# TensorE operands on 64-byte starts, and one step per hand-over between engines, in a two-stage GLU plus FFT kernel

## The chip, the core and the metric

One core of a Trainium2 chip runs one program. Its engines work in parallel and each takes its own instructions in order: TensorE (PE: matmuls, and PEld, the load of the stationary operand before each), VectorE (DVE), ScalarE (ACT), GpSimd (POOL) and SyncE (SP, which here issues nearly all DMAs; SPq is its queue). They wait for each other through semaphores. The metric is the device time of one execution in microseconds (us).

## The reference

```python
x = A_x                                     # 1 x 2048 x 576, float32
xn = layernorm(x)
# A: 2-D FFT over (2048, 576), times w_r + i w_i, and back
y = irfft2(rfft2(xn, axes=(-2, -1)) * (w_r + 1j * w_i), s=(2048, 576))
# B: gated linear unit, F = 4608
g = xn @ w_gate                             # 2048 x 4608
u = xn @ w_up
z = (sigmoid(g) * u) @ w_down               # 4608 -> 576
out = x + y + z
```

## The kernel before

**Splits.** Matmuls read float32r. A value is split in two: ACT copies it rounded (`hi`), DVE subtracts that from the value (`lo`), and a product is three matmuls, hi x hi, lo x hi, hi x lo. So nearly every operand passes from ACT to DVE to PE. The helper is `split` (L134: ACT in L135, DVE in L136).

**First stage: h = sigmoid(g) * u.** The tokens are in two halves p, the features in 36 blocks f of 128. After four blocks worked plainly, `unit(f, p)` forms g and u of one block and half by seven products of sums (a 2x2 scheme with seven multiplications), each of seven matmuls of 512 columns (L352). The moving operands lie in tiles `X0...` for p = 0 (pool x0, at the upper end of the on-chip memory, "right") and `X1...` for p = 1 (pool x1, from the lower end), the weights in `w`. In the built program every X0 tile starts 32 bytes behind a multiple of 64, every X1 tile on one. PSUM banks are A, B and E; B is copied out by ACT (L395, L401) between products, and the fourth product needs the copy of L401 to be done. Beside the matmuls, one piece at each of seven places of a unit, run: `make_w` (splits of the next weights, L205 on ACT, L207 on DVE, with differences of blocks in L227 to L231), `export` (sums of h on DVE, L429 to L438, stored to DRAM as `ss`), and `make_t` (the same for w_down: `wd` to `tP`, L455 ACT, L457 DVE, stored to DRAM as `ts`).

**Second stage: the down projection in 252 steps.** `seq` lists (j, p, k): seven products j, two halves p, 18 blocks k. Step n takes a 128x512 block `sf` from DRAM (`fetch`, ten steps ahead, in a ring of eight buffers), splits it to `sp` (`cut`, four steps ahead, six buffers) and does 12 matmuls of 288 columns (L955): for each of four token tiles m three, into PSUM tile `m`, with moving operand `tt` (24 buffers; in the built program all 32 bytes behind a multiple of 64). After the last k of a sum, `evac` adds tile m to the accumulators `acc` and `u` (L885).

**The FFT runs beside these steps** as chains, 16 in each of three phases; a chain begins every 4.4 steps (`RATE`) and goes on by one `yield` per step. Phase 1 (`phase1b`, from step 3): normalise, transposes `pf`, products `pd` (290 columns) and `pa`, out to DRAM `sc1`. Phase 2 (from step 82): load `x2`, split, products `pb` (L772), ACT copies `sw` (L774, L775), DVE multiplies with the weights (L779, L780) and adds (L781), split `zh`/`zl`, products `pc` (L790), ACT copy `u`, out to `sc2`. Phase 3 (from step 163): load, split, `py`, `pz`, `pe` (L844), added to `acc`. Two double PSUM tiles `pp` serve them all. The 290-column operands of the FFT have rows of 1160 bytes and so start at changing multiples of 8 bytes.

**Order.** The code above records instructions; the layer under it then orders them on each engine by its own plan, so what stands on an engine is not the code's order exactly.

Of the kernel before, what the change touches and what calls it, by code (L numbers as in the profile page):

```python
# [56 lines left out]
def _constants():  # L57
# [4 lines left out]
    t = np.zeros((P, 2, 5, NQ), np.float32)  # L62
    for e, v in ((0, np.cos(ang)), (1, -np.sin(ang))):
        m = np.zeros((HD + 1, NQ))
        m[:, :KD] = v
        if e == 0:
            m[HD] *= 0.5
        else:
            m[0] = m[HD] = 0.0
            m[:, 256] = m[:, 288] = 0.0  # L70
        hi, lo = _split(m)
        for part, w in ((0, hi), (1, lo)):
            t[:, e, 2 * part] = w[:P]
            t[:, e, 2 * part + 1] = w[P:2 * P]
        t[:3 * FR, e, 4] = np.concatenate([hi[2 * P:], hi[2 * P:], lo[2 * P:]])
    out["cf"] = t.reshape(P, 10 * NQ)

# [46 lines left out]
def spectral_glu_kernel(ctx: ExitStack, tc: tile.TileContext, x, w_r, w_i, w_gate, w_up, w_down, out):  # L124
# [47 lines left out]
    first = ExitStack()  # L172
    xps = [first.enter_context(tc.tile_pool(name="x0", bufs=1, side="right", reuse_waits="tile")), pool1("x1")]
# [46 lines left out]

    def make_w(f):
# [3 lines left out]
        yield from parts(new_w(f, 0, 3), raw[:, 1:])  # L225

        nc.vector.tensor_tensor(raw[:, 3::-3], raw[:, :2], raw[:, 3::-3], op=OP.subtract)  # L227
# [68 lines left out]
    def new_rem(p, c, what):  # L296
        XR[p, c] = run.tile([P, TPC, 2, 3, REM], F32R, tag="rab"[0] + "ab"[c], name=f"rm{what}{p}{c}")
# [117 lines left out]
    def export(k, p):  # L415
# [10 lines left out]
        s = run.tile([P, 3, CW], F32, tag="s", name=f"s{k}_{p}")  # L426
        S1, S2, S4 = (s[:, i] for i in range(3))
# [10 lines left out]
        nc.vector.tensor_tensor(S4, A12, S2, op=OP.subtract)  # L438
        put("P3", S4)
        yield  # L440

    def make_t(k):

        ws = []
        for i in range(2):
            w = run.tile([P, D], F32, tag="r" + "ab"[i], name=f"wd{2 * k + i}")
# [6 lines left out]
        def put(what, src):  # L453
            t = run.tile([P, 2, HD], F32R, tag="tt", name=f"t{what}{k}")
# [23 lines left out]
    nc.scalar.dma_start(f32(idr), con["id"])  # L478
# [101 lines left out]
    TS, FA, CA = NPR + 6, 10, 4  # L580
# [28 lines left out]
    for i, u in enumerate(UNITS):  # L609
# [35 lines left out]
        if p == 1:  # L645
            sides += [make_t(k) for k in range(NPR) if 4 + k * 5 // 3 == f]
# [16 lines left out]
    spp = pool2("sp")  # L663
# [26 lines left out]

    def phase1b(t):
# [10 lines left out]
        eo = pool.tile([P, 2, HD + 2], F32, tag="eo", name=f"eo{t}")  # L702
        for e, op in ((0, OP.add), (1, OP.subtract)):
            nc.vector.tensor_tensor(eo[:, e, :HD + 1], xb[:, :HD + 1], xb[:, HD:D + 1][:, ::-1], op=op)
        rp = pool.tile([P, 2, 3, FR], F32R, tag="rp", name=f"rp{t}")
        rem = eo[:, :, 2 * P:2 * P + FR]
        split(rp[:, :, 0, :], rp[:, :, 1, :], rem)
        nc.scalar.activation(rp[:, :, 2, :], rem, AF.Copy)
        yield
        yield  # L710
        pt = pair(f"pf{t}")
        for e in range(2):
            for k in range(2):
                nc.tensor.transpose(pt[:, 0, (2 * e + k) * P:(2 * e + k + 1) * P], eo[:, e, k * P:(k + 1) * P], idf)
            nc.tensor.transpose(pt[:3 * FR, 1, e * P:(e + 1) * P].bitcast(F32R), rp[:, e].rearrange("p a b -> p (a b)"), idr)
# [269 lines left out]
```

## Time and profile before

| | |
|---|---|
| times of three runs, us | 1482.88, 1485.45, 7819.09; median 1485.45 |
| profiled execution, us | 1485.09 |
| its span, us | 1483.3 (1.8 us lie around it) |
| busy: PE, PEld, DVE, ACT | 1424.0, 1232.4, 970.7, 712.2 us |
| DMA moved | 306.00 MB, 206 GB/s on average |
| first matmul of the second stage | 886.88 us from the start |

In the rows of the groups, the number after "x" is a count, then come the busy time in us, the mean duration of one in ns, and the idle time of the engine ahead of them with what ended it. Matmuls are pipelined: one that lasts 300 ns may be followed by the next after 133 ns, so the time from start to start is what counts. In the table of stretches each engine has its busy time and its count; PEclk is the granted share of TensorE's clock, "DMA share" the mean busy share of the 16 DMA engines.

### The profile page before, as it was taken

Reading aid. Unit: us, or ns where it says so; the run is one execution under the profiler, and the core shown is the slowest. Engines: PE = TensorE matmul, PEld = TensorE weight load, DVE = VectorE, ACT = ScalarE, POOL = GpSimd, SP = SyncE. Lnnn points to the kernel's source line nnn. Section 1 sums busy time; section 2 is a strip of 40 time slices with the busy share of each in tenths; the row PEclk is TensorE's granted clock in tenths of the full one; section 3 lists DMA queues with packets and bytes.
Section 4 is the critical chain, followed back from the end, with each engine's and each line's share of the span. In section 5 each row is a group of like instructions: output and inputs, shape, how many; then the busy total and the mean of one; then the engine's idle time right before and its main releaser. Section 6 shows DMA issues by size and latency. Waiting matters only on the chain. (4 is left out here: it accounts for less than half of the span.)

```text
span 1483.3 us, 22724 instructions
## 1 busy us (share of the span) xinstructions
PE 1424.0 (96%) x7804; PEld 1232.4 (83%) x7804; DVE 970.7 (65%) x1808; ACT 712.2 (48%) x1430; POOL 9.5 (1%) x36
## 2 busy tenths in 40 slices
PE   6999999999999999999999998999999988899998
PEld 4888778787777777877778778999999887899998
DVE  6877566766667666676766735666666577566663
ACT  6664344444444444444444433655555545455542
POOL 1000000000000000000000000000000000000000
PEclk9999999999999999999999999999999999999999
DMA  7234445455455554555455379988998888888862
GB/s 192 89 102 167 169 147 189 176 183 174 145 188 186 183 170 173 190 186 179 166 191 199 133 258 297 276 263 244 289 267 284 250 288 277 304 295 263 262 174 84
DMA packets 209668, 306.00 MB, mean 206 GB/s; under 512 B 20496, under 2 KB 90384, under 8 KB 209296
## 3 DMA queue, kind: packets, MB, share of 16 engines
q1 hardware_dynamic: 207344, 302.06, 61.6%
q10 hardware_dynamic: 2208, 2.49, 0.5%
q8 instruction: 61, 1.00, 0.3%
q14 instruction: 55, 0.45, 0.1%
HBM read 187.03 MB, written 117.44 MB: 205 GB/s over the span
## 5 line engine op out<-in xcount | busy, mean ns | idle before, releaser
L955 PE MATMUL m<-tt,sp 128*128 128x288 f32 x3024 | 451.7, 300 | 18.0 <-ACT sp L135 8.9
L955 PEld LDWEIGHTS m<-tt,sp 128*128 128x128 f32 x3024 | 420.9, 191 | 24.3 <-ACT sp L135 12.1
L136 DVE TENSOR_TENSOR sp<-sf,sp 128x512 fp32r<-128x512 f32 x252 | 172.3, 690 | 102.8 <-ACT sp L135 100.1
L135 ACT ACTIVATE sp<-sf 128x512 fp32r<-128x512 f32 x252 | 155.3, 628 | 91.6 <-PE m L955 71.1
L457 DVE TENSOR_TENSOR tP<-wd,tP 128x288 fp32r<-128x288 f32 x126 | 57.5, 456 | 144.6 <-ACT tP L455 143.6
L205 ACT ACTIVATE w<-raw 128x384 fp32r<-128x384 f32 x246 | 115.2, 516 | 57.7 <-DVE raw L227 37.5
L352 PE MATMUL pA<-X0A,w 128*128 128x512 f32 x518 | 137.3, 402 | 1.8 <-DVE w L207 1.1
L455 ACT ACTIVATE tP<-wd 128x288 fp32r<-128x288 f32 x126 | 55.8, 443 | 160.2 <-DMA ts<-tP 152.3
L352 PE MATMUL pA<-X1A,w 128*128 128x512 f32 x518 | 129.9, 390 | 0.0
L352 PE MATMUL pB<-X0S,w 128*128 128x512 f32 x476 | 123.2, 398 | 2.8 <-ACT pB L391 2.1
L352 PE MATMUL pE<-X0S,w 128*128 128x512 f32 x490 | 125.9, 396 | 0.0
L352 PE MATMUL pE<-X1S,w 128*128 128x512 f32 x490 | 123.7, 392 | 0.0
L352 PE MATMUL pB<-X1S,w 128*128 128x512 f32 x476 | 120.7, 393 | 1.1 <-ACT h L395 0.8
L352 PEld LDWEIGHTS pA<-X0A,w 128*128 128x128 f32 x518 | 98.2, 191 | 25.7 <-DVE w L207 1.6
L352 PEld LDWEIGHTS pA<-X1A,w 128*128 128x128 f32 x518 | 97.1, 188 | 21.2
L352 PEld LDWEIGHTS pB<-X0S,w 128*128 128x128 f32 x476 | 88.5, 188 | 27.7 <-ACT pB L391 5.2
L352 PEld LDWEIGHTS pE<-X0S,w 128*128 128x128 f32 x490 | 91.8, 188 | 22.1 <-DVE h L402 0.4
L352 PEld LDWEIGHTS pE<-X1S,w 128*128 128x128 f32 x490 | 91.9, 188 | 20.9
L352 PEld LDWEIGHTS pB<-X1S,w 128*128 128x128 f32 x476 | 89.1, 188 | 22.3 <-ACT h L395 2.4
L207 DVE TENSOR_TENSOR w<-raw,w 128x512 fp32r<-128x512 f32 (+2 forms) x108 | 82.4, 763 | 8.4 <-ACT w L205 7.7
L402 DVE TENSOR_TENSOR h<-h,pE 128x512 f32<-128x512 f32 x68 | 46.6, 685 | 61.2 <-ACT h L401 55.5
L412 DVE TENSOR_TENSOR h<-h,g 128x1024 f32<-128x1024 f32 x68 | 83.2, 1224 | 4.1
(185 smaller groups left out, 1813.4 us busy)
## 6 DMA issues: line engine op xcount, KB each, us to landing
sf<-ss SPq DMA_DIRECT2D x252, 256.0 KB
ss<-h SPq DMA_DIRECT2D x144, 256.0 KB
ts<-tP SPq DMA_DIRECT2D x126, 288.0 KB
tt<-ts SPq DMA_DIRECT2D x126, 288.0 KB
ss<-s SPq DMA_DIRECT2D x108, 256.0 KB
wd<-in_B_w_down SPq DMA_DIRECT2D x36, 288.0 KB
raw<-in_B_w_gate SPq DMA_DIRECT2D x72, 128.0 KB
raw<-in_B_w_up SPq DMA_DIRECT2D x72, 128.0 KB
```

The source lines that it names most:

```text
L135: nc.scalar.activation(hi, src, AF.Copy)
L136: nc.vector.tensor_tensor(lo, src, f32(hi), op=OP.subtract)
L205: nc.scalar.activation(o[:, i, :3, :], src[:, i], AF.Copy)
L207: nc.vector.tensor_tensor(o[:, :, 3:, :], src[:, :, :KT, :], f32(o[:, :, :KT, :]), op=OP.subtract)
L352: nc.tensor.matmul(b, w[:, sw, :], xx[:, sx, :], start=start and j == 0, stop=stop and j == len(STEPS) - 1, skip_group_check=skip)
L402: nc.vector.tensor_tensor(h[:, 1], h[:, 1], bE, op=OP.add)
L412: nc.vector.tensor_tensor(h, h, g, op=OP.mult)
L455: nc.scalar.activation(t[:, 0], src, AF.Copy)
L457: nc.vector.tensor_tensor(t[:, 1], src, f32(t[:, 0]), op=OP.subtract)
L955: nc.tensor.matmul(o, s[:, a, m * P:(m + 1) * P], t[:, b, :], start=k == 0 and i == 0, stop=k == NPR - 1 and i == 2)
```

## The change

It has five parts.

1. **Starts.** Tiles are padded so that all operands of TensorE start at multiples of 64 bytes: the FFT's rows of 290 columns get a pitch `NP` = 304, odd small tiles are rounded up, and a tile `edge` of 32 bytes shifts everything that is allocated from the upper end (X0, `tt`, `sf`).
2. **Hand-overs.** In the chains ACT's part, DVE's part and PE's part of each split stand in steps of their own (a `yield` between), where before ACT and DVE had one step and PE the next but one. `cut` becomes `cut_hi` (four steps ahead) and `cut_lo` (three). Chains begin every 4.36 steps, from steps 2, 83 and 166.
3. **First sums.** `early`, which runs beside the last units of the first stage, now also splits the first five blocks (`sp` lies in the same pool as `sf`). The ring `sf` has six buffers in place of eight.
4. **Weights and w_down.** `make_w` puts the differences and the second and third group's ACT copies ahead of their DVE parts; `tP` (tag `tt`) has two buffers in place of one; `make_t` begins a block every 8/5 feature blocks in place of 5/3. These tiles move to the upper pool `brief`. `export` reuses A12 in place of a third buffer.
5. **Twins.** At the first and the last block of each sum the matmuls of two steps are taken tile by tile together, so that the tiles m of one sum end 6 matmuls apart.

```diff
+NP = 304
...
-    idf = fix.tile([P, P], F32, name="idf")
     idr = fix.tile([P, P], F32R, name="idr")
+    idf = f32(idr)
+    ctx.enter_context(tc.tile_pool(name="edge", bufs=1, side="right")).tile([P, 8], F32, name="edge")
...
     def make_w(f):
...
-        yield from parts(new_w(f, 0, 3), raw[:, 1:])
+        w0 = new_w(f, 0, 3)
+        yield from high(w0, raw[:, 1:])
+        low(w0, raw[:, 1:])
+        yield
         nc.vector.tensor_tensor(raw[:, 3::-3], raw[:, :2], raw[:, 3::-3], op=OP.subtract)
         yield
-        yield from parts(new_w(f, 1, 2), raw[:, ::3])
         nc.vector.tensor_tensor(B22, B22, B11, op=OP.subtract)
         nc.vector.tensor_tensor(B21, B21, B22, op=OP.subtract)
-        yield
-        yield from parts(new_w(f, 2, 2), raw[:, 1:3])
+        w1 = new_w(f, 1, 2)
+        yield from high(w1, raw[:, ::3])
+        w2 = new_w(f, 2, 2)
+        yield from high(w2, raw[:, 1:3])
+        low(w1, raw[:, ::3])
+        yield
+        low(w2, raw[:, 1:3])
...
-            t = run.tile([P, 2, HD], F32R, tag="tt", name=f"t{what}{k}")
+            t = brief.tile([P, 2, HD], F32R, tag="tt", name=f"t{what}{k}", bufs=2)
...
-            SF[n] = s = ring.tile([P, CW], F32, tag="sf", name=f"sf{n}", bufs=8)
+            SF[n] = s = ring.tile([P, CW], F32, tag="sf", name=f"sf{n}", bufs=FS)
...
     def early():
         for k in range(NPR):
             fetch_t(0, k)
-            if k % 2 == 0 and k // 2 < 8:
+            if k % 2 == 0 and k // 2 < FS:
                 fetch(k // 2)
+            if k >= 12:
+                if k - 12 <= CA:
+                    cut_hi(k - 12)
+                if 0 <= k - 13 < CA:
+                    cut_lo(k - 13)
             yield
...
     def phase2(i):
...
         yield
         yield
-        h = pool.tile([P, 2, NQ], F32R, tag="x2h", name=f"x2h{i}")
-        l = pool.tile([P, 2, NQ], F32R, tag="x2l", name=f"x2l{i}")
-        split(h, l, x2)
-        yield
+        h, l = wide("x2h", i, 1, F32R), wide("x2l", i, 1, F32R)
+        hi(h, x2)
+        yield
+        lo(l, x2, h)
         yield
         pb = pair(f"pb{i}")
...
+        yield
+        sw, z, t2 = wide("sw", i), wide("z", i, 2), wide("t2", i)
...
-        nc.vector.tensor_tensor(z, z, t2, op=OP.add)
-        zh, zl = zz[i % len(zz)]
-        split(zh[:, :, :KD], zl[:, :, :KD], z)
-        yield
-        yield
+        nc.vector.tensor_tensor(z[:, :, :KD], z[:, :, :KD], t2[:, :, :KD], op=OP.add)
+        yield
+        zh, zl = R["zz"]
+        hi(zh[:, :, :KD], z[:, :, :KD])
+        yield
+        lo(zl[:, :, :KD], z[:, :, :KD], zh[:, :, :KD])
         yield
         pc = pair(f"pc{i}")
...
-            add(c11, u)
+            add(c11, v)
...
-    RATE = 4.4
-    B1, B2, B3 = 3, 82, 163
+    RATE = 4.36
+    B1, B2, B3 = 2, 83, 166
...
     for n, (j, p, k) in enumerate(seq):
-        for q in range(8, FA + 1) if n == 0 else (n + FA,):
-            fetch(q)
+        fetch(n + FA)
...
-        cut(n + CA)
+        if n:
+            cut_hi(n + CA)
+            cut_lo(n + CA - 1)
+        twin = k in (0, NPR - 2)
         for m in range(TPC):
+            if k not in (1, NPR - 1):
+                down(n, m)
+            if twin:
+                down(n + 1, m)
```

How it moves instructions, at three places. First DVE at the end of the first stage, before: `sp` is the split of a first block, L402 to L412 are the last units' h, L429 to L438 the sums of `export`.

```order
L411 TENSOR_TENSOR h_1_7646<-h_1_7646,pE_1_7649 128x512
L867 MEMSET zh 128x2
L867 MEMSET zl 128x2
L412 TENSOR_TENSOR h_1_7646<-h_1_7646,g_1_7647 128x1024
L429 TENSOR_TENSOR s_1_7713<-h_1_7530,h_1_7646 128x512
L432 TENSOR_TENSOR s_1_7713<-s_1_7713,h_1_7530 128x512
L435 TENSOR_TENSOR h_1_7530<-h_1_7530 128x512
L438 TENSOR_TENSOR s_1_7713<-h_1_7646,s_1_7713 128x512
L136 TENSOR_TENSOR sp_7750<-sf_7544,sp_7750 128x512
L136 TENSOR_TENSOR sp_7753<-sf_7562,sp_7753 128x512
```

The same place after the change (L621 is `cut_lo`, L423 to L433 are the h of the last units, L450 to L456 the last sums):

```order
L621 TENSOR_TENSOR sp_7669<-sf_7584,sp_7669 128x512
L433 TENSOR_TENSOR h_1_7536<-h_1_7536,g_1_7537 128x1024
L621 TENSOR_TENSOR sp_7682<-sf_7601,sp_7682 128x512
L423 TENSOR_TENSOR h_1_7655<-h_1_7655,pE_1_7658 128x512
L621 TENSOR_TENSOR sp_7695<-sf_7617,sp_7695 128x512
L432 TENSOR_TENSOR h_1_7655<-h_1_7655,pE_1_7658 128x512
L621 TENSOR_TENSOR sp_7810<-sf_7633,sp_7810 128x512
L433 TENSOR_TENSOR h_1_7655<-h_1_7655,g_1_7656 128x1024
L928 MEMSET zh 128x2x15
L928 MEMSET zl 128x2x15
L450 TENSOR_TENSOR s_1_7737<-h_1_7536,h_1_7655 128x512
```

The first six blocks' lower parts now stand ahead of the last sums; before they stood behind them.

Second, ACT in phase 2, before (L774/L775 `sw` of one chain, then `zh` of it; `sp` are splits for later steps):

```order
L774 ACTIVATE sw_11344<-pb_11337 64x578
L775 ACTIVATE sw_11344<-pb_11337 64x578
L135 ACTIVATE sp_11437<-sf_11263 128x512
L135 ACTIVATE sp_11455<-sf_11286 128x512
L135 ACTIVATE zh<-z_11347 128x2x289
L792 ACTIVATE u_11419<-pc_11412 128x580
L135 ACTIVATE sp_11493<-sf_11320 128x512
```

and after (L825/L826 `sw`, L722 the rounded copies of the chains, L617 `cut_hi`):

```order
L825 ACTIVATE sw_11380<-pb_11349 64x2x289
L826 ACTIVATE sw_11380<-pb_11349 64x2x289
L722 ACTIVATE u_11405<-pc_11373 128x2x290
L617 ACTIVATE sp_11445<-sf_11278 128x512
L722 ACTIVATE zh<-z_11381 128x2x289
L617 ACTIVATE sp_11471<-sf_11309 128x512
```

One or two splits stand between `sw` and `zh`, as before; but on PE the matmuls between the last of `pb` and the first of `pc` of the same chain are now 30 to 68 (44 on average of 16 chains), before 22 to 42 (33).

Third, PE at a change of sum in phase 3, before, where `m_00` to `m_03` are the tiles of the ending sum:

```order
L955 MATMUL m_00_14167<-tt_16_14089,sp_14539 128x288 x3
L955 MATMUL m_01_14171<-tt_16_14089,sp_14539 128x288 x3
L955 MATMUL m_02_14175<-tt_16_14089,sp_14539 128x288 x3
L955 MATMUL m_03_14179<-tt_16_14089,sp_14539 128x288 x3
L955 MATMUL m_00_14167<-tt_17_14125,sp_14556 128x288 x3
L955 MATMUL m_01_14171<-tt_17_14125,sp_14556 128x288 x3
```

and after:

```order
L1008 MATMUL m_00_14124<-tt_16_14049,sp_14494 128x288 x3
L1008 MATMUL m_00_14124<-tt_17_14108,sp_14517 128x288 x3
L1008 MATMUL m_01_14131<-tt_16_14049,sp_14494 128x288 x3
L1008 MATMUL m_01_14131<-tt_17_14108,sp_14517 128x288 x3
L1008 MATMUL m_02_14138<-tt_16_14049,sp_14494 128x288 x3
L1008 MATMUL m_02_14138<-tt_17_14108,sp_14517 128x288 x3
```

Each tile of the sum is now complete six matmuls after the one ahead of it, and the next sum's first two steps stand in pairs as well.

More of the change, by code (lines that the diff above doesn't have):

```diff
@@ L72, in _constants @@
         for part, w in ((0, hi), (1, lo)):
[L73 to L76, printed above, removed]
+            t[:, e, 2 * part, :NQ] = w[:P]
+            t[:, e, 2 * part + 1, :NQ] = w[P:2 * P]
+        t[:3 * FR, e, 4, :NQ] = np.concatenate([hi[2 * P:], hi[2 * P:], lo[2 * P:]])
+    out["cf"] = t.reshape(P, 10 * NP)
     s1 = np.arange(N1)
@@ L172, in spectral_glu_kernel @@
     first = ExitStack()
+    brief = first.enter_context(tc.tile_pool(name="brief", bufs=1, side="right", reuse_waits="tile"))
     xps = [first.enter_context(tc.tile_pool(name="x0", bufs=1, side="right", reuse_waits="tile")), pool1("x1")]
@@ L194, in load_raw @@
         cols = slice(f * P, (f + 1) * P)
-        RAW[f] = raw = run.tile([P, 4, 3, P], F32, tag="raw", name=f"raw{f}", bufs=2)
+        RAW[f] = raw = brief.tile([P, 4, 3, P], F32, tag="raw", name=f"raw{f}", bufs=2)
         for src, blks in ((w_gate, (3, 2)), (w_up, (0, 1))):
@@ L219, in weight, with high, low @@
         return WS[f, i][:, n]
+    def high(o, src):
+        for i in range(o.shape[1]):
+            nc.scalar.activation(o[:, i, :3, :], src[:, i], AF.Copy)
+            yield
+    def low(o, src):
+        nc.vector.tensor_tensor(o[:, :, 3:, :], src[:, :, :KT, :], f32(o[:, :, :KT, :]), op=OP.subtract)
+        r = slice(REM, 2 * REM)
+        nc.vector.tensor_tensor(o[r, :, KT, :], src[r, :, KT, :], f32(o[r, :, KT, :]), op=OP.subtract)
     def make_w(f):
@@ L296, in new_rem @@
     def new_rem(p, c, what):
-        XR[p, c] = run.tile([P, TPC, 2, 3, REM], F32R, tag="rab"[0] + "ab"[c], name=f"rm{what}{p}{c}")
+        XR[p, c] = brief.tile([P, TPC, 2, 3, REM], F32R, tag="rab"[0] + "ab"[c], name=f"rm{what}{p}{c}")
     def rem_parts(p, c, m):
@@ L425, in export @@
         put("P4", A22)
-        s = run.tile([P, 3, CW], F32, tag="s", name=f"s{k}_{p}")
-        S1, S2, S4 = (s[:, i] for i in range(3))
+        s = run.tile([P, 2, CW], F32, tag="s", name=f"s{k}_{p}")
+        S1, S2 = (s[:, i] for i in range(2))
         yield
@@ L645, in spectral_glu_kernel @@
         if p == 1:
-            sides += [make_t(k) for k in range(NPR) if 4 + k * 5 // 3 == f]
+            sides += [make_t(k) for k in range(NPR) if 4 + k * 8 // 5 == f]
     finish(*sides)
@@ L689, in landed, with hi, lo, wide @@
             put(t, slice(HD, D) if first_rows else slice(0, D))
+    def hi(o, src):
+        nc.scalar.activation(o, src, AF.Copy)
+    def lo(o, src, h):
+        nc.vector.tensor_tensor(o, src, f32(h), op=OP.subtract)
+    def wide(name, t, bufs=1, dtype=F32):
+        return R["pool"].tile([P, 2, NP], dtype, tag=name, name=f"{name}{t}", bufs=bufs)[:, :, :NQ]
+    def left_over(name, t):
+        r = R["pool"].tile([P, 2, 112], F32R, tag=name, name=f"{name}{t}")[:, :, :3 * FR]
+        return r, r.rearrange("p e (a b) -> p e a b", a=3)
     def phase1b(t):
@@ L789, in phase2 @@
             for n, (k, m) in enumerate(((2, zh), (2, zl), (3, zh))):
-                nc.tensor.matmul(pc[:, j, :NQ], bm[:, k, :], m[:, j, :], start=n == 0, stop=n == 2)
-        u = pool.tile([P, 2, NQ], F32, tag="u", name=f"u{i}", bufs=2)
-        nc.scalar.activation(u, pc[:, :, :NQ], AF.Copy)
+                nc.tensor.matmul(pc[:, j, :NQ], bm[:, k, :], m[:, j, :NQ], start=n == 0, stop=n == 2)
+        yield
+        u = wide("u", i, 2)
+        hi(u, pc[:, :, :NQ])
         nc.sync.dma_start(sc2.rearrange("(p kl) n -> p kl n", kl=N2)[:, kl:kl + 2], u)
@@ L796, in phase3 @@
         pool, di = R["pool"], R["di"]
-        u = pool.tile([P, 2, NQ], F32, tag="u3", name=f"u3{t}", bufs=2)
+        u = wide("u3", t, 2)
         nc.sync.dma_start(u, sc2[2 * t * P:(2 * t + 2) * P].rearrange("(j p) n -> p j n", j=2))
@@ L804, in phase3 @@
         yield
-        uh = pool.tile([P, 2, NQ], F32R, tag="uh", name=f"uh{t}")
-        ul = pool.tile([P, 2, NQ], F32R, tag="ul", name=f"ul{t}")
-        split(uh, ul, u)
+        uh, ul = wide("uh", t, 1, F32R), wide("ul", t, 1, F32R)
+        hi(uh, u)
         yield
+        lo(ul, u, uh)
         yield
@@ L855, in stage1 @@
         pool = room("1")
-        R["cf"] = cf = pool.tile([P, 2, 5, NQ], F32R, name="cf")
+        R["cf"] = cf = pool.tile([P, 2, 5, NP], F32R, name="cf")
         load_r(cf, con["cf"].rearrange("p (e k n) -> p e k n", e=2, k=5))
@@ L872, in stage3 @@
         pool = room("3")
-        R["di"] = di = pool.tile([P, 2, 5, NQ], F32R, name="dit")
+        R["di"] = di = pool.tile([P, 2, 5, NP], F32R, name="dit")
         load_r(di, con["di"].rearrange("p (e k n) -> p e k n", e=2, k=5))
```

168 lines of the change are left out of this document (91 added, 77 removed).

## The prediction

> **What bounds the kernel now.** I read the page's totals, then the stretches, then the waits.
>
> ```profile
> span 1483.3 us, 22724 instructions
> PE 1424.0 (96%) x7804; PEld 1232.4 (83%) x7804; DVE 970.7 (65%) x1808; ACT 712.2 (48%) x1430; POOL 9.5 (1%) x36
> core 0: us, PE busy (x) PEld busy (x) DVE busy (x) ACT busy (x) POOL busy (x), PEclk, DMA share, GB/s
> 38.00:887.00 849.00, 835.36 (x3653) 668.74 (x3652) 568.56 (x975) 383.86 (x784) 2.71 (x6) 1.00 0.49 171
> 887.00:933.00 46.00, 39.32 (x268) 37.77 (x266) 28.40 (x53) 20.17 (x43) 0.40 (x4) 0.93 0.95 302
> 933.00:1091.00 158.00, 156.10 (x1130) 149.49 (x1131) 103.12 (x203) 90.33 (x196) 1.09 (x11) 1.00 0.87 267
> 1091.00:1141.00 50.00, 49.45 (x362) 48.11 (x360) 30.75 (x61) 24.99 (x41) 0.00 (x0) 1.00 0.94 285
> 1141.00:1283.00 142.00, 122.85 (x812) 114.47 (x811) 97.23 (x210) 71.57 (x122) 0.00 (x0) 0.95 0.83 267
> 1283.00:1454.00 171.00, 171.00 (x1301) 170.87 (x1301) 107.31 (x207) 91.53 (x193) 0.00 (x0) 1.00 0.80 258
> ```
>
> PE bounds it: 96% busy. The stretches are the start of the program's body: first stage (38 to 887 us), then the second stage's first steps with FFT phase 1 (to 1091), phase 2 (to 1283), phase 3 (to 1454). Phase 3 has no idle PE at all. Phase 2 has, and there two others come near: the DMA engines are busy 0.83 of the time and DVE 97 of 142 us.
>
> A busy PE can still be slow, so the time from start to start comes next: stage one on a tile of each pool, then phase 3 (timeline of PE; pieces of the chain that ended last).
>
> ```profile
> 852.08 3.43 PE L352 MATMUL pE<-X0S,w 128*128 128x512 f32 x14
> 855.35 1.80 PE L352 MATMUL pB<-X0S,w 128*128 128x512 f32 x7
> ...
> 874.75 3.34 PE L352 MATMUL pE<-X1S,w 128*128 128x512 f32 x14
> ...
> 877.93 1.78 PE L352 MATMUL pB<-X1S,w 128*128 128x512 f32 x7
> ...
> 1331.44 1.87 PE pe L844 x14
> 1334.12 3.20 PE m L955 x24
> ```
>
> 14 matmuls take 855.35 - 852.08 = 3.27 us on X0, 233.6 ns each, and 3.18 us on X1, 227.1 each: same shape, same weights, 6.5 ns apart. In phase 3 a 288-column matmul takes 3.20 / 24 = 133.3 ns, a 290-column one 1.87 / 14 = 133.6.
>
> One reading fits all four. Count the 64-byte blocks that a row of the moving operand touches. 512 columns are 2048 bytes: 32 blocks in X1; 33 in X0, which starts 32 bytes into a block. 227.1 / 32 = 7.10 ns, 233.6 / 33 = 7.08. 288 columns are 1152 bytes and `tt` starts 32 bytes in: 19 blocks, 133.3 / 19 = 7.02. 290 columns are 1160 bytes, 19 blocks at every start that is a multiple of 8: 7.03. It is a fit, not a proof.
>
> **The change part by part.** The sum is made against the profiled execution, 1485.1 us (span 1483.3 and 1.8 around it); the median of the runs, 1485.45, lies 0.35 above.
>
> *Starts, X0.* This row counts L352 alone:
>
> ```profile
> 38.00:887.00 849.00, 824.73 (x3506) 653.98 (x3506) 1.00 0.49 171
> ```
>
> Half of 3506, 1753, read X0; 1753 x 6.5 ns = **11 us**. Nothing waits for anything else there, so it counts in full. Ends: 0 if the difference is the half's and not the start's, 11.
>
> *Starts, tt.* By the fit an aligned 288-column matmul touches 18 blocks, 126.3 ns, 7 less.
>
> ```profile
> L955 PE MATMUL m<-tt,sp 128*128 128x288 f32 x3024 | 451.7, 300 | 18.0 <-ACT sp L135 8.9 <-DVE sp L136 8.6 <-DVE u L885 0.4
> ```
>
> 3024 x 7 = 21 us if PE alone bounds. The same line by stretches:
>
> ```profile
> 1141.00:1283.00 142.00, 105.30 (x662) 95.06 (x661) 0.95 0.83 267
> 1283.00:1454.00 171.00, 127.63 (x899) 121.81 (x899) 1.00 0.80 258
> 1454.00:1483.00 29.00, 22.92 (x171) 22.59 (x169) 0.97 0.18 52
> ```
>
> From 1283 on it does: 1070 matmuls, 7.5 us. Up to 1141 the other 1292 run beside DMA shares of 0.87 to 0.95; I take 4 of 9 us. In the rest of phase 2 nothing. **11 us**, ends 0 and 21. The FFT's 290 columns stay at 19 blocks: nothing.
>
> The Trainium skill, TensorE: Matmul & The Clock Gate, "Back-to-back issue gap", gives the warm gap as N / 2.4 + 2.5 ns, by the column count alone: 215.7 ns at 512. The rows differ at one N and lie above it; by the page both terms of the starts would be zero. That speaks against this part, and is a rival below.
>
> *Weights and `tP`.* The list of waits, and an instance:
>
> ```profile
> ACT tP L455 <- DMA ts<-tP: 152.3, 85, 4.8
> ACT w L205 <- DVE raw L227: 37.5, 29, 2.5
> PEld pB L352 <- ACT h L401: 19.7, 25, 2.0
> 818.59 0.45 ACT L455 ACTIVATE tP<-wd 128x288 fp32r<-128x288 f32 x1 [4.79 <-DMA ts<-tP]
> 818.94 0.58 ACT L408 ACTIVATE g<-pB 128x512 f32<-128x512 f32 x1
> ```
>
> With one `tP` buffer ACT sits until the store has landed, and the copies that PE needs queue behind it. PE is idle 849.0 - 835.4 = 13.6 us in this stretch; by starts, 3506 at 230.4 ns and the 147 transposes, taken at 133 ns like a 290-column matmul, leave 22. Two buffers take away the first row; the second stays in part, since ACT's order still has `w` between two of the copies. I take **11 us**, the half; ends 0 and 20, as part of the rest is no wait of these two.
>
> *First sums.* The timeline at the change of stage:
>
> ```profile
> 885.99 3.22 ACT L135 ACTIVATE sp<-sf 128x512 fp32r<-128x512 f32 x6
> ...
> 887.87 1.23 DVE L412 TENSOR_TENSOR h<-h,g 128x1024 f32<-128x1024 f32 x1
> 889.13 0.69 DVE L429 TENSOR_TENSOR s<-h,h 128x512 f32<-128x512 f32 x1
> ...
> 891.07 0.69 DVE L438 TENSOR_TENSOR s<-h,s 128x512 f32<-128x512 f32 x1
> 891.67 3.70 DVE L136 TENSOR_TENSOR sp<-sf,sp 128x512 fp32r<-128x512 f32 x6
> 892.41 7.73 PEld L955 LDWEIGHTS m<-tt,sp 128*128 128x128 f32 x40 [5.33 <-DVE sp L136]
> ```
>
> DVE does the last h and four sums before the first lower parts; PE waits 5.1 to 5.3 us and then runs at a lower clock (0.93 in 887:933, some 3 us). In the changed order six lower parts stand ahead. Next late is the DMA, at 0.95 in this stretch. **6 us**, ends 2 and 8.
>
> *Hand-overs in phase 1 and its last steps (933 to 1141).* 1130 and 362 matmuls at 133.5 ns are 151 and 48.3 us of 158 and 50, so at most 9 us. What comes late instead: by the new order, `sf` of these steps is issued only 66 to 170 matmuls ahead of its use, before mostly 150 to 220, since six buffers free later and SP, in order, holds every later load behind that wait. 66 x 133 ns = 8.8 us against a landing of 6.76 us (the row is below). **4 us**, ends -6 and 9.
>
> *Hand-overs in phase 2 (1141 to 1283).* 812 x 133.5 ns = 108.4 us of 142: **33.6 us** lost. One chain:
>
> ```profile
> 1184.19 3.22 PE L955 MATMUL m<-tt,sp 128*128 128x288 f32 x23
> ...
> 1185.11 0.65 ACT L775 ACTIVATE sw<-pb 64x578 f32<-64x578 f32 x1
> ...
> 1188.00 0.76 DVE L781 TENSOR_TENSOR z<-z,t 128x578 f32<-128x578 f32 x1
> ...
> 1188.85 0.69 ACT L135 ACTIVATE zh<-z 128x578 fp32r<-128x578 f32 x1 [1.92 <-DVE z L781]
> ...
> 1189.59 0.40 PE L790 MATMUL pc<-zh,bmt 128*128 128x290 f32 x1 [2.18 <-ACT zh L135]
> ```
>
> From the end of `pb` (1184.3) to `zh` ready is 5.2 us, 39 matmuls; 24 stood between. The new order has 44 on average but 30 to 33 in four of 16 chains, so this wait shrinks and does not end. ACT still stands at `zh` behind one or two `sp`; while it waits, the splits behind it wait. The floor is the DMA: 0.83 x 142 = 118 us of full work, and the highest share of a whole stretch is 0.95, so 124 us. **16 us** of the 18 that this leaves, as `sf` and `x2` are issued earlier here than before. Ends -5 and 24.
>
> The Trainium skill, DMA: Bandwidth & Descriptors, "Where 436 GB/s comes from", puts the HBM limit of a core at about 358 GB/s; this stretch moves 142 x 267 = 37.9 MB, 106 us by that, which would leave PE the bound. The rows show 302 GB/s at a share of 0.95, so 318 at most.
>
> *Edits at nothing.* Twins: the evacuations had cost PE 0.4 us in all (L885 in the row of L955); DVE hides them. `idf` and `idr` in one, a P1 sum from PSUM, two buffers for `z` and S3 in place: under DVE's 65%. Without that cover each is under 1 us. `make_t`'s new pace moves ACT work of the first stage, 45% busy. The strided `x2` and `u` halve the runs of 32 DMAs; their cost is in phase 2's range.
>
> Sum: 11 + 11 + 11 + 6 + 4 + 16 = 59; 1485.1 - 59 = **1426 us**.
>
> **The rivals.** *A, starts give nothing*: the 6.5 ns belong to the units of p = 0, and 133 ns is a bound of the weights' load, which is busy 170.87 of 171 us in phase 3. 1426 + 22 = 1448. The fit of four rows speaks against it; the skill's rule would end here. *B, the DMA holds the second stage*: at 0.95 in 887:933 and 0.94 in 1091:1141 it is nearly full, and a faster PE asks for more. Of 26 us and the 4 of `tt` some 5 stay: 1451. *C, the hand-overs are undone by the ordering layer*: ACT's order in phase 2 reads nearly as before. Phase 1 and 2 give 1 in place of 20: 1445. *D, all waits go*: phase 1 and first steps at a share of 0.95 are 190.7 in place of 204 (13), phase 2 gives 18, phase 3 8, first stage 31: 1415; at a share of 1.0, 1399. *E, slower: the ring of six.*
>
> ```profile
> SPq L793 <- ACT u L792: 55.1, 14, 6.5
> L136 DVE TENSOR_TENSOR sp<-sf,sp 128x512 fp32r<-128x512 f32 x252 | 172.3, 690 | 102.8 <-ACT sp L135 100.1
> L135 ACT ACTIVATE sp<-sf 128x512 fp32r<-128x512 f32 x252 | 155.3, 628 | 91.6 <-PE m L955 71.1
> 1090.80 6.76 DMA sf<-ss
> ```
>
> A buffer's round is landing 6.76, split 0.63 and 0.69, one step of some 2.1 for the later lower part, and SP held by up to 6.5: 16.7 us for six steps, 2.78 per step. The mean step now is (1483 - 887) / 252 = 2.37 us; above six of these, 14.2 us, the ring takes over from PE. Over 163 steps of phases 1 and 2 it would be 453 us in place of 396; less 11 + 11 + 7.5, 1512. For it: SP did wait that long. Against: the new order gives `sf` 80 matmuls or more in phase 2.
>
> **How the numbers follow.** My forecast, 1412 to 1440, 0.42; A 0.12; B 0.14; C 0.14; D 0.13; E 0.05. A, B, C and D below 1456 are faster by over 2% (about what a measurement of this kernel can tell from no change): 0.86 with the forecast, as misses of two kinds together pass it. Within 2% 0.11, slower by over 2% 0.03. The range 1398 to 1453 takes in A to D and leaves out E and their sums.
>
> **What would show it.** X0 and X1 both at 227 ns (starts); 288 columns at 126 against 290 at 133 (the fit); no wait of `tP` on its store; no PE gap at the change of stage; 1141:1283's work in about 126 us at a DMA share near 0.95. The prediction fails if phase 1 shows new PE waits on `sp` or `xb`, or SP holds fetches.

## The result, and the profile after

| | before | changed |
|---|---|---|
| median of four runs on one chip, us | 1484.28 | 1470.44 |
| profiled execution's span, us | 1483.3 | 1469.0 |
| first matmul of the second stage, us from the start | 886.88 | 887.19 |
| from there to step 82 / 82 to 108 / 108 to 162 / 162 to the end, us | 204.6 / 49.1 / 139.1 / 203.5 | 205.6 / 48.5 / 124.2 / 203.5 |

The ratio is 0.9908, interval 0.9891 to 0.9925. The forecast was 1426, its range 1398 to 1453, so the time lies above it: of the 59 us of the sum, 14 came. A step is timed from its first matmul; step 162 opens a pair that the changed kernel takes tile by tile (part 5 of the change), so the first matmul of step 163 comes nine matmuls sooner there and would be no fair mark. (One run of before took 7819 us; comparisons leave it out.)

Totals and stretches of the changed kernel, with the columns of the table of before:

```profile
span 1469.0 us, 22700 instructions
PE 1409.5 (96%) x7804; PEld 1225.3 (83%) x7804; DVE 963.7 (66%) x1808; ACT 707.7 (48%) x1430; POOL 9.5 (1%) x36
...
38.00:620.00 582.00, 564.12 (x2495) 451.23 (x2494) 412.82 (x757) 281.99 (x588) 2.61 (x5) 1.00 0.55 188
620.00:887.00 267.00, 266.31 (x1156) 216.16 (x1155) 153.55 (x222) 105.74 (x199) 0.10 (x1) 1.00 0.38 132
887.00:933.00 46.00, 40.29 (x286) 39.25 (x285) 23.41 (x44) 17.11 (x37) 0.30 (x3) 0.93 0.93 286
933.00:1091.00 158.00, 151.12 (x1105) 145.38 (x1104) 102.43 (x206) 85.58 (x194) 1.19 (x12) 1.00 0.84 263
1141.00:1266.00 125.00, 114.94 (x803) 108.98 (x801) 93.00 (x204) 69.28 (x119) 0.00 (x0) 0.99 0.98 293
```

Phase 2 does 803 matmuls in 125 us, at a DMA share of 0.98; before, 812 took 142 us. This part came out near the forecast. The first stage is busy 830.4 of 849 us, before 835.4, and 933 to 1091 holds 1105 matmuls, before 1130: there nothing came.

PE's timeline at the end of the first stage, the place shown of before:

```profile
852.53 3.43 PE L373 MATMUL pE<-X0S,w 128*128 128x512 f32 x14
855.79 1.79 PE L373 MATMUL pB<-X0S,w 128*128 128x512 f32 x7
...
875.11 3.33 PE L373 MATMUL pE<-X1S,w 128*128 128x512 f32 x14
878.28 1.75 PE L373 MATMUL pB<-X1S,w 128*128 128x512 f32 x7
```

14 matmuls take 3.26 us on X0, 232.9 ns each, and 3.17 on X1, 226.4: X0 now starts at a multiple of 64 and is as slow as before.

The waits of the changed kernel, engines first, then SyncE's queue:

```profile
ACT tP L476 <- DMA ts<-tP: 86.6, 63, 4.4
PEld pB L373 <- ACT h L422: 24.7, 22, 2.1
```

```profile
SPq L442 <- DVE h L433: 140.3, 39, 11.0
SPq L133 <- PE pa L791: 44.7, 12, 4.4
```

ScalarE's stand at `tP` fell from 152.3 us to 86.6, and still PE waits longer for `h` (24.7 us; 19.7 before). The last row is new in this size (13.3 us before): SyncE stands at the load of `am`.

The changed kernel's timelines behind the change of stage (PE, VectorE, SyncE):

```profile
913.28 0.69 PE L759 MATMUL pf<-idr,eo 128*128 128x128 f32 x2 [5.31 <-DVE eo L747]
```

```profile
912.08 0.58 DVE L294 TENSOR_SCALAR xb<-xb,mv,rstd 128x576 f32<-128x576 f32 x1 [9.21 <-DMA xb<-in_A_x]
```

```profile
898.92 0.45 SPq L133 DMA_DIRECT2D cf<-c_cf  x1
...
900.36 2.07 SPq L146 DMA_DIRECT2D xb<-in_A_x  x2
```

The gap of 5.1 to 5.3 us at the change of stage is gone, and 13 steps later PE stands 5.31 us at the first `pf`. The first `xb` was issued at 901.1 us before and is at 900.4 now, and VectorE could begin on it at 911.2 us before and at 912.1 now; PE merely comes there sooner. So a part of the gain is lost again: from step 0 to 36 it is 88.5 us, before 90.9, and from step 36 to 108 it is 165.6, before 162.8.

### The profile page after: what moved, and what is told of

Same layout as the page of the kernel before. It is cut to its first block, busy times and chain, and to the rows that moved or that the text cites. A ratio compares the mean times of both kernels' runs of the same rounds, so it can differ in the third digit from the quotient of the medians.

```text
span 1469.0 us, 22700 instructions
## 1 busy us (share of the span) xinstructions
PE 1409.5 (96%) x7804; PEld 1225.3 (83%) x7804; DVE 963.7 (66%) x1808; ACT 707.7 (48%) x1430; POOL 9.5 (1%) x36
## 4 chain that ended last, share of the span: by engine, by line
PE 51%; DVE 15%; DMA 15%; ACT 5%; issue 4%; SPq 4%; DVEq 0%; ACTq 0%
PE m L1008 17%; PE pB L373 11%; PE pE L373 7%; DMA ts<-tP 7%; PE pA L373 7%; DMA sf<-ss 2%; PE pd L778 2%; PE pe L903 2%; DVE w L231 2%; DVE h L433 2%; DMA ss<-h 2%; DVE tP L478 1%; SPq L205 1%; ACT ah L722 1%; DVE w L233 1%
## 5 line engine op out<-in xcount | busy, mean ns | idle before, releaser
L1008 PE MATMUL m<-tt,sp 128*128 128x288 f32 x3024 | 435.5, 298 | 10.7 <-ACT sp L617 7.6
L1008 PEld LDWEIGHTS m<-tt,sp 128*128 128x128 f32 x3024 | 412.1, 189 | 17.2 <-ACT sp L617 11.2
L621 DVE TENSOR_TENSOR sp<-sf,sp 128x512 fp32r<-128x512 f32 x252 | 169.6, 687 | 73.4 <-ACT sp L617 70.3
L617 ACT ACTIVATE sp<-sf 128x512 fp32r<-128x512 f32 x252 | 153.5, 627 | 96.4 <-PE m L1008 48.0
L227 ACT ACTIVATE w<-raw 128x384 fp32r<-128x384 f32 x238 | 111.1, 516 | 49.4 <-DVE raw L243 33.5
L478 DVE TENSOR_TENSOR tP<-wd,tP 128x288 fp32r<-128x288 f32 x126 | 56.7, 455 | 89.9 <-ACT tP L476 88.8
L476 ACT ACTIVATE tP<-wd 128x288 fp32r<-128x288 f32 x126 | 55.2, 442 | 108.1 <-DMA ts<-tP 86.6
L416 ACT ACTIVATE h<-pB 128x512 f32<-128x512 f32 x68 | 40.4, 594 | 131.0 <-PE pB L373 123.3
L423 DVE TENSOR_TENSOR h<-h,pE 128x512 f32<-128x512 f32 x68 | 46.5, 684 | 73.4 <-ACT h L422 73.1
L432 DVE TENSOR_TENSOR h<-h,pE 128x512 f32<-128x512 f32 x68 | 46.4, 683 | 72.4 <-PE pE L373 72.4
```

Of the source, the lines that this page charges most:

```text
L227: nc.scalar.activation(o[:, i, :3, :], src[:, i], AF.Copy)
L416: nc.scalar.activation(h[:, 0], bB, AF.Copy)
L423: nc.vector.tensor_tensor(h[:, 1], h[:, 1], bE, op=OP.add)
L432: nc.vector.tensor_tensor(h[:, 0], h[:, 0], bE, op=OP.add)
L476: nc.scalar.activation(t[:, 0], src, AF.Copy)
L478: nc.vector.tensor_tensor(t[:, 1], src, f32(t[:, 0]), op=OP.subtract)
```

## The experiments

Ratios are to the kernel before, run on the same chip; the changed kernel's is 0.991. Chips differ by some us, so ratios are compared. Where the end of the first stage is compared, each figure is one profiled execution: the changed kernel, e4, e7, e11 and e12, whose first stage is the same, end it at 887.2, 887.2, 889.4, 888.1 and 888.6 us, so a difference under 2.2 us says nothing.

### Why X0 is slower than X1

**e1, e2: other starts.**

```diff
e1 -    ... .tile([P, 8], F32, name="edge")
   +    ... .tile([P, 24], F32, name="edge")
e2 +    xps[1].tile([P, 16], F32, name="pad")
```

> The changed kernel with an edge tile of 96 bytes in place of 32: X0, tt, sf and sp start at multiples of 128 bytes (before the change 96 past one, in the changed kernel 64 past one; X1 is at a multiple of 128 in both). Theory 1, a start at a multiple of 128 is what the 227 ns need: X0 goes from 233 to 227 ns per matmul, 11 us; if tt follows the same step of some 6.5 ns, another 8 to 20 us: 1440 to 1460 us. Theory 2, the 6.5 ns belong to the half p = 0 or its place and not to the start: X0 stays at 233, 288 columns at 133, the time at 1470 within 3 us.

> The changed kernel with a tile of 64 bytes ahead of X1, so that X1 starts 64 bytes past a multiple of 128, as X0 does. Theory 1 (multiples of 128 decide): X1 goes from 227 to 233 ns, as slow as X0, and the time to 1481 us. Theory 2 (the half or its place decides): X1 stays at 227, the time at 1470 within 3 us.

e1: 0.9887 (0.986 to 0.9913), X0 at 232.8 ns on average. e2: 0.9899 (0.9875 to 0.9923), X1 at 229.0. Theory 1 fell: neither start made X0 fast or X1 as slow as X0.

**e5, e6, e10: the place, the rows, the unit.**

```diff
e5  -    side="right" / side="left" of every pool
    +    exchanged, with pads that keep each start modulo 128
e6  -    rows(x, tid(p, c, m))            # in stage_x
    +    rows(x, tid(1 - p, c, m))
e10 +    p = 1 - p if 4 <= f < NF - 2 else p    # in made()
```

> The changed kernel with every pool on the other side of SBUF: X0 at 24384 to 96064 in place of 134464 to 206144, X1 at 96384 to 168064 in place of 62336 to 134016, each at the same place within 128 bytes as before. Theory P, the place in SBUF decides: X0 falls to 227 ns, or X1 rises to 233. Theory H, what the half p = 0 itself brings (its rows, or its units' place in the order) decides: X0 stays at 233.3 and X1 at 227 ns. The time is 1470 to 1475 us either way.

> The changed kernel in which the first stage takes the other half's rows of x for each p (only the rows are exchanged; the output is that of other rows). Theory V, the values of the rows decide: X0 goes to 227 ns and X1 to 233. Theory U, the unit or its place decides: X0 stays at 233.3, X1 at 227. The time is 1470 to 1475 us either way.

> The changed kernel in which every unit (f, p) of f = 4 to 33 reads the X of the other half, all else in place (the rows of the output are exchanged there). Theory X, the 6 ns are tied to the tiles of X0: 233.3 ns wherever X0 is read, now in the units of p = 1. Theory U, they are tied to the units of p = 0 (their place in the order, their weights' and PSUM's buffers): X0 then takes 227 to 229 ns and X1 233 in these units, and the old values in the others.

All three single runs took 1469.6 to 1469.7 us, with X0 at 233.3 ns and X1 at 228; in e10 X0 stayed slow in the units that now read it. So it was the tile, and neither its place, its contents nor its reader.

**e13: the distance.** What e5 had kept without intent was how X lies to the weights. Set out by the distance of the moving operand's start from the stationary one's, modulo 256 bytes (addresses from the built programs, mean time from start to start of neighbours on one tile, stalls left out):

| kernel, tile | start mod 128 | distance mod 256 | ns |
|---|---|---|---|
| before, X1 with the first two weight tiles | 0 | 0 | 228.3 |
| before, X1 with the third | 0 | 128 | 232.6 |
| before, X0 | 96 | 224 and 96 | 233.3 and 233.7 |
| changed and e5, X1 | 0 | 0 | 228.0 |
| changed and e5, X0 | 64 | 192 | 233.3 |
| e1, X0 | 0 | 128 | 232.8 |
| e2, X1 | 64 | 64 | 229.0 |

```diff
-    ... .tile([P, 8], F32, name="edge")
+    ... .tile([P, 56], F32, name="edge")
```

> The changed kernel with an edge tile of 224 bytes in place of 32: X0 then starts at a distance from the weights that is a multiple of 256 bytes, as X1 does (192 over one in the changed kernel; tt and sp move together, their distance stays). Theory M, the distance modulo 256 decides: X0 falls from 233.3 to 228 ns, 1753 x 5.3 = 9 us, a ratio to the kernel before of 0.984 to 0.986 in place of 0.991. Theory O, something else in the tiles of X0: 233.3 stays, 0.990 to 0.992.

0.9828 (0.9809 to 0.9846). PE's timeline of e13, the same place:

```profile
846.84 3.34 PE L373 MATMUL pE<-X0S,w 128*128 128x512 f32 x14
850.01 1.75 PE L373 MATMUL pB<-X0S,w 128*128 128x512 f32 x7
...
869.05 3.33 PE L373 MATMUL pE<-X1S,w 128*128 128x512 f32 x14
872.22 1.75 PE L373 MATMUL pB<-X1S,w 128*128 128x512 f32 x7
```

Now both take 3.17 us for 14, 226.4 ns. e1 and e13 start X0 at the same place modulo 128; one gave nothing, the other the gain. Their starts modulo 256 differ as well, but the start alone does not decide. X1 of the kernel before and X0 of e1 both start at multiples of 256; the first took 228.3 ns with weights at multiples of 256 and 232.6 with weights 128 bytes past one, the second 232.8 with weights 128 past. On average X0 fell by 5.8 ns, to 227.5, and X1, unmoved, by 1.0: (5.8 + 1.0) x 1753 = 12 us of matmul time. Not all of it reached the end of the stage, which in e13 is here:

```profile
881.14 19.07 PE L1008 MATMUL m<-tt,sp 128*128 128x288 f32 x143
```

That is 6.1 us sooner than in the changed kernel (887.19): from 56 us on, starts that come over 70 ns late add up to 26.5 us there and to 31.8 in e13, so a part of the 12 went into longer waits. The profiled execution is 8.5 us shorter in all; that the ratio fell by 0.008, about 12 us, is no check of the 12. Why the distance counts no run shows.

### Why the first stage did not gain

Each late matmul between 56 and 886 us was followed back to the copy it waited for, and along that engine's queue to the instruction that stood at its head. Before, 4.1 us stood behind `tP` on ScalarE and 8.0 behind `w`; after, 13.7 behind `tP` on ScalarE and 5.2 behind `w`, of 26.4 us in all. Such a count says where a wait stood, not what its removal is worth; the runs below show how far the two differ.

**e3, e8, e9: `tP` and the stores elsewhere.**

```diff
e3 -            nc.sync.dma_start(ssp[ORDER.index(what)][p][k], src)
   +            nc.gpsimd.dma_start(ssp[ORDER.index(what)][p][k], src)
e8 -            nc.scalar.activation(t[:, 0], src, AF.Copy)
   +            nc.gpsimd.tensor_copy(t[:, 0], src)
e9      as e8, and the lower part, the differences and the store ts on nc.gpsimd
```

> The changed kernel with the stores of h and its sums (ss) issued by GpSimd in place of SyncE. Theory S, SyncE in order is held by these stores while they wait for h, and the stores of tP and the first loads of the second stage stand behind them: the wait of ACT tP on ts<-tP (86.6 us in the changed kernel) falls below 45, PE loses 4 to 8 us less in the first stage, the first pf's wait of 5.3 us falls below 2: 1457 to 1463 us. Theory L, the landing itself is what tP waits for, and the first pf waits for a full DMA: both waits stay within a fifth, 1470 within 3 us.

> The changed kernel with GpSimd in place of ScalarE making the upper part of tP, so that ScalarE never waits for a store of tP. Theory T, ScalarE's stand of 86.6 us at tP is what makes h late for PE in the first stage: PE's wait on ACT h L422 (24.7 us of the weight loads, 15.6 of the matmuls) falls by half or more, PE is busy 570 us or more of 38 to 620 in place of 564, and the time falls by 6 to 12 us. Theory W, other waits of ScalarE (w on raw, 33.5 us) and the order itself hold h: PE gains under 2 us. The cost of GpSimd's copy of 128x288 is not seen in any trace of these kernels; if it is over 3 us, make_t runs late and the time rises.

> The changed kernel with all of make_t on GpSimd: both parts of tP, the differences of the blocks, and the stores ts, so that neither ScalarE nor VectorE nor SyncE stands at a tP any more. Theory T, what PE loses in the first stage behind stands at tP (13.7 of 26.4 us between 56 and 886 us, traced back through ScalarE's queue) is the price of those stands: PE is busy 574 us or more of 38 to 620 in place of 564, and the ratio to the kernel before falls from 0.991 to 0.981 to 0.984. Theory W, a stand elsewhere (w on raw) takes its place as in the run with only the upper parts on GpSimd: PE stays at 564 or below, 0.991 or above. GpSimd's copy took 0.58 us in that run; its subtraction has not been seen.

All slower than the changed kernel: 1.013 (1.0103 to 1.0157), 0.9987 (0.9977 to 0.9996), 1.0709 (1.069 to 1.0728). Waits of e3, e8 and e9, the last with its SyncE:

```profile
ACT tP L476 <- DMA ts<-tP: 111.5, 71, 4.4
DVE h L459 <- DMA ss<-h: 43.3, 19, 3.7
```

```profile
POOL tP L476 <- DMA ts<-tP: 305.8, 93, 14.3
DVE tP L478 <- POOL tP L476: 76.8, 42, 4.6
```

```profile
DVE h L459 <- DMA ss<-h: 140.4, 19, 25.5
PE pE L373 <- DVE h L423: 112.0, 14, 22.6
```

```profile
SPq L468 <- POOL tP L478: 238.3, 34, 15.6
```

In e3 SyncE is free of the stores of `h`, and `tP` waits longer for its own, 111.5 us in place of 86.6: theory S fell, and theory L too, as the time rose. In e8 ScalarE no longer stands at `tP`, but GpSimd does, and VectorE behind it, 76.8 us (88.8 behind ScalarE in the changed kernel); PE's weight loads wait longer for `h`, 33.7 us in place of 24.7, so theory T fell. In e9 no engine but GpSimd stands at `tP`, but a block there takes longer (its subtraction 918 ns, its copy 546), SyncE stands 238 us at the next load of `wd`, the store of A12 queues behind it, and VectorE, which forms S3 in A12's place, stands until that store has landed: PE stands 112 us behind it. So S3 in A12's place comes into question.

**e14, e17, e18: parts of the change undone.**

```diff
e14 -    ... name=f"t{what}{k}", bufs=2)      and    4 + k * 8 // 5 == f
    +    ... name=f"t{what}{k}")              and    4 + k * 5 // 3 == f
e17      make_w as before
e18      e14, and
    -        nc.vector.tensor_tensor(A12, A12, S2, op=OP.subtract)
    +        nc.vector.tensor_tensor(S4, A12, S2, op=OP.subtract)
```

> The changed kernel with make_t's part undone: tP in one buffer, the old pace (a block every 5/3 f in place of 8/5). Traced back through ScalarE's queue, PE lost 4 us behind stands at tP before the change and 13.7 after, behind w 8.0 and 5.2. Theory B, the second buffer lets the order put copies of tP ahead of the copies of h that PE needs, and their stands cost what w's gain brought: the first stage ends 4 to 9 us earlier, a ratio of 0.985 to 0.988. Theory N, the stands only change their place: within 2 us, 0.990 to 0.992.

> The changed kernel with make_w as before (each group of upper parts followed at once by its lower parts and the differences between them; all else as changed). Theory G, the new make_w costs the first stage what the second buffer of tP brings, as it puts six upper copies and both differences of raw in a row ahead of the lower parts: the stage ends 3 to 6 us earlier, a ratio of 0.986 to 0.989 in place of 0.991. Theory K, the new make_w helps, as the stands at w fell from 8.0 to 5.2 us: the stage ends 2 to 5 us later, 0.992 to 0.995; what costs the first stage is then S3 in A12's place or the pace, not tried.

> The changed kernel with tP in one buffer at the old pace, as in e14, and S3 in a plane of its own, as before the change. Theory Q, S3 in the place of A12 costs the first stage, since VectorE stands until A12's store has landed: that wait (18.7 us in e14) goes, the first stage ends 4 to 6 us earlier than in e14, a ratio of 0.989 to 0.991 in place of 0.994. Theory R, VectorE's stands there are off PE's path: as e14, 0.993 to 0.995.

0.9936 (0.9917 to 0.9954), 0.9926 (0.991 to 0.9943), 0.9885 (0.9856 to 0.9915). The first matmuls of the second stage in the changed kernel, e14, e17 and e18, and a wait of e14:

```profile
887.19 12.98 PE L1008 MATMUL m<-tt,sp 128*128 128x288 f32 x97
```

```profile
892.94 7.29 PE L1008 MATMUL m<-tt,sp 128*128 128x288 f32 x54
```

```profile
889.32 10.86 PE L1001 MATMUL m<-tt,sp 128*128 128x288 f32 x81
```

```profile
887.36 12.85 PE L1008 MATMUL m<-tt,sp 128*128 128x288 f32 x96
```

```profile
DVE h L459 <- DMA ss<-h: 18.7, 8, 3.0
```

The second buffer with its pace is worth 892.94 - 887.19 = 5.7 us, or 3.5 against e7's 889.4. S3 in A12's place costs 892.94 - 887.36 = 5.6, give or take the 2.2, where `tP` has one buffer; in e18 this wait is not in the list. `make_w`'s order is not shown to bring anything: e17 ends the stage 2.1 us later, as e7 does, its ratio's interval overlaps the changed kernel's, and VectorE's wait on the store of A12 rose in it as well, to 26.4 us. So theory B of e14 and theory G of e17 fell, and theory Q of e18 held: a gain and a loss of about one size. With two buffers the loss was not measured, as the on-chip memory has no room for a third plane beside them. The wait is smaller there, so the loss may be too; in the changed kernel:

```profile
DVE h L459 <- DMA ss<-h: 9.2, 9, 2.0
```

### Phase 1

**e4, e7, e11.**

```diff
e4  -    xb ... bufs=2, three yields, begin at base + int(t * RATE)
    +    xb ... bufs=3, five yields, begin two steps earlier (t > 0)
e7  -    am ... bufs=2
    +    am ... bufs=4
e11 +    am and xb in three buffers, eo in two; xb one step earlier, norm one step
    +    earlier against pf; cf loaded behind the first xb
```

> The changed kernel with xb and am of every chain of phase 1 but the first loaded two steps earlier, xb in three buffers, the rest of the chain where it was. Theory X, the lead of xb (47 to 70 matmuls, less than its landing) is what pf waits for: the waits of pf in chains 2 to 16 (0.4 to 1 us each) fall to nearly nothing, 5 to 8 us: 1462 to 1465 us. Theory D, the DMA is full, and an earlier xb makes sf later by as much: pf's waits become waits on sp, 1470 within 3 us.

> The changed kernel with four buffers for am in place of two. A chain of phase 1 now has 14 steps at a spacing of 4.36, so over three chains are open at once, and SyncE waits 40.5 us in 11 times (933 to 1141 us) for pa of the chain two before, with sf and xb queued behind. Theory A, this wait is what phase 1 loses: the wait goes, pf no longer waits for xb, 933 to 1091 us holds 1130 matmuls or more in place of 1105: 4 to 9 us less than the changed kernel, a ratio to the kernel before of 0.985 to 0.988 in place of 0.991. Theory D, the DMA is the bound (a share of 0.84 to 1.03 there): the waits move to sf, the ratio stays at 0.991.

> The changed kernel with phase 1 arranged for its longer chain: am in three buffers, xb in three, eo in two; xb of chains 2 to 16 issued one step earlier and normalised one step earlier, ahead of the lower parts of the chain two before; the first chain's xb issued ahead of cf. Theory N, the losses of phase 1 are VectorE's order (the next xb's normalisation stands behind al, which waits for ah and pd) and the first xb behind cf: the 4 to 5.5 us at the first pf fall below 2, the ten waits of 0.8 us go: 6 to 10 us, a ratio of 0.984 to 0.987. Theory D, the DMA at a share of 0.84 to 1.03 holds these steps anyway: under 3 us, 0.989 to 0.991.

e4: 0.9942 (0.9921 to 0.9963), and 933 to 1091 us holds 1052 matmuls, 1105 in the changed kernel. Its SyncE, 933 to 1141 us:

```profile
SPq L133 <- PE pa L790: 54.9, 13, 6.4
```

`am`, loaded with `xb`, waits for `pa` of the chain two before, 40.5 us there in the changed kernel and 54.9 here, and the later loads stand behind it. So neither of its theories was met. e7: 0.9909 (0.9894 to 0.9924). The wait is gone and nothing came, as its theory D had it: SyncE now stands at the store of `x1` (26.9 us, 7.0 in the changed kernel) and the loads of `sf` (25.6, there 13.9), and `pf` still waits 14 times for `eo`, 14.8 us in place of 17.7. Around the fifth chain's in e7, VectorE:

```profile
956.42 1.40 DVE L725 TENSOR_TENSOR al<-pd,ah 64x290 fp32r<-64x290 f32 x3 [3.39 <-ACT ah L722]
957.74 0.57 DVE L294 TENSOR_SCALAR xb<-xb,mv,rstd 128x576 f32<-128x576 f32 x1
```

It stands 3.39 us at `al` of an earlier chain, and the next chain's `xb` is queued behind: the new steps put them in that order. e11: 0.9874 (0.9859 to 0.9889); the first `pf` and its stretch:

```profile
908.70 0.38 PE L759 MATMUL pf<-idr,eo 128*128 128x128 f32 x2
```

```profile
887.00:933.00 46.00, 41.69 (x300) 39.75 (x299) 26.23 (x50) 18.82 (x42) 0.48 (x6) 1.00 1.02 310
```

Its stall of 5.3 us is gone, and steps 2 to 18 take 35.8 us in place of 39.8. But the DMA share there is now 1.02, steps 18 to 36 take 48.6 in place of 45.6, and from step 0 to 162 it is 375.7 us in place of 378.3: 2.6 us. Theory N named the stalls rightly, theory D what was left of the gain. That the DMA took the rest back is read from its share; no run frees the DMA to show it. Nor does any run change VectorE's order alone: e11 also adds buffers and moves loads.

### Phase 2

**e12.**

```diff
         hi(h, x2)
-        yield
         lo(l, x2, h)
...      (and the four other new yields of phase2)
```

> The changed kernel without the five steps that the change added to a chain of phase 2 (after the upper parts of x2h, after pb, within z, after zh, after pc); phase 1 and 3, x2's load and the strided tiles as changed. Theory H, these steps are what took phase 2 from 142 to 125 us: the stretch from step 108 to 163 goes back to 138 to 142 us, a ratio of 1.000 to 1.003. Theory L, the earlier loads of x2 and sf did it: it stays below 130, a ratio of 0.991 to 0.994.

1.003 (1.0018 to 1.0043): the whole gain of the change is gone. Steps 108 to 162 take 139.7 us (124.2 with the steps, 139.1 before). Counted to the first matmul of step 163, as the expectation does, it is 141.3, 125.1 and 142.1. Theory H held.

```profile
1141.00:1266.00 125.00, 109.35 (x697) 100.19 (x697) 83.50 (x179) 61.87 (x102) 0.00 (x0) 0.95 0.90 268
```

697 matmuls in place of 803 in this time.

### Together

**e15, e16:** e11 with e13's edge; the same with e14's single buffer.

> The changed kernel with phase 1 mended (am and xb in three buffers, eo in two, xb one step earlier and ahead of cf) and X0 at distance 0. If both add up: 0.9874 x 0.994 = 0.981 to 0.983; if phase 1 gives the gain of the first stage back to the DMA: 0.985 or above.

> As the run before, with tP in one buffer at the old pace too. By theory B of that part 4 to 9 us less than the run before, 0.976 to 0.979; by theory N the same as the run before.

0.9824 (0.9806 to 0.9843) and 0.9892 (0.9877 to 0.9906). e15 beats both kernels, but is not told apart from e13 alone: phase 1 shows no gain on top. The second buffer again proves worth its place: without it e16's first stage ends at 890.1 us, e15's at 880.6, 9.5 us apart.

## Why the prediction was wrong

Behind each term stand its size in the sum and what the runs showed, in us. By stages the profiled execution is 14.3 us shorter: the first stage 0.3 longer, steps 0 to 36 2.4 shorter, 36 to 108 2.7 longer, 108 to 162 14.9 shorter, and the rest as before.

- **Starts, X0 (11, measured 0) and tt (11, measured 0).** The step that failed is the fit to 64-byte blocks, 22 of the 45 us that are missing. It met four rows out of many; the trace of before also held X1 with the third weight tile, on a multiple of 64 and at 232.6 ns, which no count of blocks gives. What decides at 512 columns is the distance to the weights. Rival A's outcome came; its first reason, the units of p = 0, fell with e10 and e13, and its second, a bound by the weights' load, no run tests. For `tt` the distance went from 96 and 224 (134.0 and 131.6 ns) to 0 and 128 (132.5 and 134.0), which on average is no gain: from step 162 on, where PE hardly waits, it is 203.5 us before and after. So 288 columns do not follow the order of the 512. The Trainium skill, TensorE: Matmul & The Clock Gate, "Back-to-back issue gap", gives N / 2.4 + 2.5 ns, 215.8 at 512 (the prediction wrote 215.7), as the gap of an isolated matmul, and about 131 ns at 512 for a stream of weight loads and matmuls; in neither does the operand's start count. The runs agree that multiples of 64 by themselves bring nothing, but 226.4 and 232.9 ns stand at one count here, above both.
- **Weights and tP (11, measured 0.3 the other way).** The stand at `tP` was a right one and the half was too much: by e14 the second buffer brought 3.5 to 5.7, and by e17 `make_w`'s order nothing that can be told from the spread. What was missed is S3 "in place", priced under 1 us by VectorE's busy share. A share says nothing of a wait: the edit made VectorE wait for a store, and e18 prices that at 5.6 with one `tP` buffer. X1's third weight tile, now at distance 0, should have brought 477 x 4.6 ns = 2 us more. Together that would be 0 to 2 us of gain; the stage ended 0.3 us later, within the spread of 2.2.
- **First sums (6, measured 2.4 up to step 36).** The gap went, as said. "Next late is the DMA" was the right warning and was not priced: the first `xb` lands no earlier, and 5.3 us reappear at `pf`.
- **Hand-overs of phase 1 (4, measured -2.7 from step 36 to 108).** The loss lies within the stated ends. The fear named was the six-buffer ring. What came was the longer chain: VectorE works in order, and `al` of one chain stands ahead of the next `xb`, so `pf` waits; new waits on `xb` were the sign of failing that the prediction named.
- **Hand-overs of phase 2 (16, measured 14.9).** Right in what the new steps do (e12), and right in size. The floor behind the size is not shown: the DMA was busy 0.98 x 125 = 122.5 us and not 118, at a share above the 0.95 taken as its most, and the two errors nearly cancel. PE's waits from 1141 to 1266 us name ScalarE's `sp` first (5.7 us) and no DMA.
- **Rivals.** C fell with e12. E fell too: steps 0 to 162 take 378.3 us, where it put 453 on the first 163. D fell with the waits that are still there. B left 5 us of gain to the second stage, and 14.6 came; that most of e11's gain went again at a DMA share of 1.02 speaks for its reason in phase 1, phase 2's 14.9 us against it.

## What to carry to other kernels

A fit that meets the rows it was made from is a guess: before an edit rests on it, sort all instructions of that form by the quantity in question, and look for the row that breaks it. A wait that goes is a gain only if the next arrival on that path is early enough; look up when it lands. Forming a result in the place of one that is being stored adds a wait on that store, whatever the engine's busy share.

## What was not expected of the hardware

Matmuls of 512 float32r columns took 226.4 to 228.3 ns from start to start where the moving operand's start lay a multiple of 256 bytes from the weights', 229.0 at 64, and 232.6 to 233.7 at 96, 128, 192 and 224. By the ratios, an edge tile of 224 bytes in place of 32 brought nearly as much again as the whole change (0.9828 against 0.9908); by the profiled executions 8.5 us against 14.3. The 288-column matmuls, at 131.6 to 134.0 ns, were not fastest at 0.
